# Attention into a gated feed-forward block on one core: token sums one by one on VectorE, one batch's last tokens earlier, two sigmoids ahead of two copies

## The chip, the cores and the metric

One Trainium2 chip, of which the kernel uses one core. The metric is the device time of one execution in microseconds (us). Engines are called as the profile calls them: PE is TensorE (PEld its weight loads), DVE is VectorE, ACT is ScalarE, POOL is GpSimd, and SP is SyncE, which here only issues DMA. Each engine works through its own instructions in program order; where the text says that an instruction stands "ahead of" another, this order on one engine is meant.

## The reference

Linear attention over 8 batches of 576 tokens with 8 heads of 64, a normalisation, and then a gated feed-forward block over all 4608 tokens of width 512.

```python
kv  = einsum('bhsd,bhse->bhde', k, v)              # per batch and head, 64x64
out = einsum('bhsd,bhde->bhse', q, kv)
x   = out / sqrt(mean(out*out) + 1e-6) * g_norm    # then as 4608 tokens x 512

g, val   = x @ w_gate, x @ w_val                   # 512 -> 1536
ffn_out  = (gelu(g) * val) @ w_out                 # 1536 -> 512
res_gate = sigmoid(x @ w_res)                      # 512 -> 512
result   = x + res_gate * ffn_out
```

## The kernel before

The feed-forward work goes in blocks of 512 tokens. Block b (0 to 7) holds the first 512 tokens of batch b; the last 64 tokens of all eight batches together make block 8. While PE works on block b, the attention of batch b+1 is done beside it. `plans[blk][slot]` lists what is added behind a slot of a block; slots 0 to NF-1 (NF = 12) are the gate and value products, NF and NF+1 the residual gates, NF+2 and NF+3 the two halves of the output product.

The output product of a block is done by a scheme with seven half-size products instead of eight (Strassen's, in Winograd's form). Each `prod` is 12 matmuls of 128x256 columns into a PSUM bank. "A", "D", "E" and "F" are banks; bank A takes four products one after the other and is read in between.

```python
def first_two():                               # slot NF+2
    prod(w["A"], a_of(blk, 1, 1), b_of(1, 1), True)
    nc.scalar.copy(out=w["E"], in_=w["A"])
    prod(w["D"], s_[0], wo_t[:, 0], True)
    nc.scalar.copy(out=w["d"], in_=w["D"])
    for j in range(NJ):
        m_sigmoid(j)                           # ACT: th = 0.5*th + 0.5

def pf(jj, src):                               # the gate: res = th * src, on DVE
    nc.vector.tensor_tensor(out=res_all[part(jj)], in0=th_all[part(jj)], in1=src, op=ALU.mult)

def fin(jj):                                   # the residual: res = res + t, on POOL
    nc.gpsimd.tensor_tensor(out=res_all[of], in0=res_all[of], in1=t_t[blk][of], op=ALU.add)

def others():                                  # slot NF+3
    prod(w["A"], s_[1], wo_t[:, 1], False)
    sub(nc.vector, w["F"], w["A"], w["d"], ALU.add)      # the sum into F
    prod(w["E"], a_of(blk, 1, 2), b_of(2, 1), False)
    pf((0, 0), w["E"])
    for f in rest:                                       # what the plan adds, all here
        f()
    prod(w["A"], s_[2], wo_t[:, 2], False)
    c22 = res_all[part((1, 1))]
    sub(nc.vector, c22, w["A"], w["d"], ALU.add)         # the sum out of A
    prod(w["F"], s_[3], b_of(2, 2), False)
    pf((0, 1), w["F"])
    fin((0, 0))
    prod(w["A"], a_of(blk, 2, 2), wo_t[:, 3], False)     # the last product
    pf((1, 1), c22)
    pf((1, 0), w["A"])
    fin((0, 1)); store(0); fin((1, 1)); fin((1, 0)); store(1)
```

In blocks 7 and 8 the gate and value products are done by the same scheme (`gv_group`, three groups of four column tiles each). It needs four sums and differences of quarters of the transposed tokens. They are made on DVE during the block before, among its output products:

```python
def token_sums(blk, eng):        # tile ts, 128x512 fp16 each; x_quadrant reads xT
    return [
        lambda: one(0, (0, 1), (0, 0)),    # used by product 5
        lambda: one(1, (1, 1), 0),         # reads sum 0; used by product 6
        lambda: one(2, (1, 1), (0, 1)),    # used by product 7
        lambda: one(3, (1, 0), 1),         # reads sum 1; used by product 4
    ]
# order of the words in a group: product 1g 1v, seed, 5g ... 6g ... plus F (DVE), 2g 2v, 7g, ...
```

The last 64 tokens of batches 2, 3, 5 and 7 (each with those of its partner) are scaled by `a_t` (DVE, o times the inverse root), multiplied by g in `a_x` (DVE) and sent through a transposing DMA (`d_xT`, SP queue):

```python
if rem:
    at(m, NF + 3, lambda: a_t(b, NJ))                    # m = b - 1; behind `others` of block m
...
if rem:
    at(m, NF + 3, lambda: a_x(b, NJ), lambda: d_xT(b, NJ, NJ + 1))
```

The last block has an output product of its own, with bank A split over two banks (`wa`):

```python
for e in range(2):
    prod(wa[e], a_of(blk, 1, 1), b_of(1, 1), True, (e,))
    nc.scalar.copy(out=we[:, one[e], :], in_=wa[e])
prod(wd, s_[0], wo_t[:, 0], True)
nc.scalar.copy(out=d, in_=wd)
for j in (2, 3, 0, 1):
    m_sigmoid(j)
for e in range(2):
    prod(wa[e], s_[1], wo_t[:, 1], False, (e,))
    sub(nc.vector, wf[:, one[e], :], wa[e], d[:, one[e], :], ALU.add)
sub(nc.gpsimd, u, th_all[part(2, 2, 1)], d, ALU.mult)              # u on POOL: tokens j = 2, 3
sub(nc.gpsimd, u, u, t_t[blk][part(2, 2, 1)], ALU.add)
prod(we, a_of(blk, 1, 2), b_of(2, 1), False)
gated(0, 2, 0, we)                       # DVE: res = th * src
plus(0, 2, 0, nc.gpsimd)                 # POOL: res = res + t
store(0, 2, 0, CH)
prod(wf, s_[3], b_of(2, 2), False)
gated(0, 2, 1, wf); plus(0, 2, 1, nc.gpsimd); store(0, 2, CH, C)
for e in range(2):
    prod(wa[e], s_[2], wo_t[:, 2], False, (e,))
    gated(2 + e, 1, 1, wa[e])
sub(nc.vector, res_all[of], res_all[of], u, ALU.add)               # DVE, reads u
store(2, 2, CH, C)
for e in range(2):
    prod(wa[e], a_of(blk, 2, 2), wo_t[:, 3], False, (e,))
    gated(2 + e, 1, 0, wa[e]); plus(2 + e, 1, 0, nc.vector)
store(2, 2, 0, CH)
```

Of the kernel before, what the change touches and what calls it, by code (L numbers as in the profile page):

```python
# [18 lines left out]
def kernel(  # L19
# [15 lines left out]
    nc = tc.nc  # L35
    P = nc.NUM_PARTITIONS
    B, H, S, D = q.shape
# [386 lines left out]
    def sub(eng, out_, in0, in1, op=ALU.subtract):  # L424
        eng.tensor_tensor(out=out_, in0=in0, in1=in1, op=op)  # L425
# [32 lines left out]
                    skip_group_check=True,  # L458
                )

    def out_by_products(blk, later, banks, rest=()):
        w = {}
        s_ = hid_sums

        def res(jj):
            for j in (2 * jj, 2 * jj + 1):
                m_res(blk, j, banks[j])

        def first_two():
            for n in ("D", "E", "F", "A"):  # L470
                w[n] = pmoe.tile([P, 2, CH], FP32, name="w" + n, bank=banks[n])
            w["d"] = finp.tile([P, 2, CH], FP32, tag="wd", bufs=1, name="wd")
# [7 lines that stand above are left out]
        def part(jj):  # L480
            return slice(None), slice(2 * jj[0], 2 * jj[0] + 2), slice(jj[1] * CH, (jj[1] + 1) * CH)

        def pf(jj, src):
            nc.vector.tensor_tensor(out=res_all[part(jj)], in0=th_all[part(jj)], in1=src, op=ALU.mult)  # L484

        def fin(jj):
            of = part(jj)
            nc.gpsimd.tensor_tensor(out=res_all[of], in0=res_all[of], in1=t_t[blk][of], op=ALU.add)  # L488

        def store(jj):  # L490
            dst = out[blk * S : blk * S + M0, :].rearrange("(p j) c -> p j c", j=NJ)
            js = slice(2 * jj, 2 * jj + 2)
            nc.sync.dma_start(out=dst[:, js, :], in_=res_all[:, js, :])

        def others():


            prod(w["A"], s_[1], wo_t[:, 1], False)
            sub(nc.vector, w["F"], w["A"], w["d"], ALU.add)
            prod(w["E"], a_of(blk, 1, 2), b_of(2, 1), False)  # L500
            pf((0, 0), w["E"])
            for f in rest:
                f()
            prod(w["A"], s_[2], wo_t[:, 2], False)
            c22 = res_all[part((1, 1))]
            sub(nc.vector, c22, w["A"], w["d"], ALU.add)
            prod(w["F"], s_[3], b_of(2, 2), False)
            pf((0, 1), w["F"])
            if not later:
                fin((0, 0))  # L510
            prod(w["A"], a_of(blk, 2, 2), wo_t[:, 3], False)
            pf((1, 1), c22)
            pf((1, 0), w["A"])
            if later:

                return
            fin((0, 1))
            store(0)
            fin((1, 1))
            fin((1, 0))  # L520
            store(1)

        if later:
            at(blk + 1, 5, lambda: fin((0, 0)))
            at(blk + 1, 6, lambda: fin((0, 1)), lambda: store(0))
            at(blk + 1, 9, lambda: fin((1, 0)))
            at(blk + 1, 10, lambda: fin((1, 1)), lambda: store(1))
        return [lambda: res(0), lambda: res(1), first_two, others]

    def out_last(blk, banks):  # L530

        s_ = hid_sums

        def bank(n, i):
            return pmoe.tile([P, n, CH], FP32, name="w", bank=i)

        def part(j, n, ch):
            return slice(None), slice(j, j + n), slice(ch * CH, (ch + 1) * CH)

        def gated(j, n, ch, src):  # L540
            of = part(j, n, ch)
            nc.vector.tensor_tensor(out=res_all[of], in0=th_all[of], in1=src, op=ALU.mult)

        def plus(j, n, ch, eng):
            of = part(j, n, ch)
            eng.tensor_tensor(out=res_all[of], in0=res_all[of], in1=t_t[blk][of], op=ALU.add)

        def store(j, n, c0, c1):
            for e, queue in enumerate((nc.sync, nc.scalar)):
                dst = out.rearrange("(j e s) c -> e s j c", e=2, s=S)[e, M0:S, j : j + n, c0:c1]  # L550
                queue.dma_start(out=dst, in_=res_all[e * R : (e + 1) * R, j : j + n, c0:c1])

        def run():
            wa = [bank(1, banks["A"][e]) for e in range(2)]
            wd, we, wf = [bank(2, banks[n]) for n in "DEF"]
            d = finp.tile([P, 2, CH], FP32, tag="wd", bufs=1, name="wd")
            u = attnp.tile([P, 2, CH], FP32, tag="sq", name="u")
            one = (slice(0, 1), slice(1, 2))
            for e in range(2):
                prod(wa[e], a_of(blk, 1, 1), b_of(1, 1), True, (e,))  # L560
                nc.scalar.copy(out=we[:, one[e], :], in_=wa[e])
            prod(wd, s_[0], wo_t[:, 0], True)
            nc.scalar.copy(out=d, in_=wd)
            for j in (2, 3, 0, 1):
                m_sigmoid(j)
            for e in range(2):
                prod(wa[e], s_[1], wo_t[:, 1], False, (e,))
                sub(nc.vector, wf[:, one[e], :], wa[e], d[:, one[e], :], ALU.add)
            sub(nc.gpsimd, u, th_all[part(2, 2, 1)], d, ALU.mult)
            sub(nc.gpsimd, u, u, t_t[blk][part(2, 2, 1)], ALU.add)  # L570
            prod(we, a_of(blk, 1, 2), b_of(2, 1), False)
            gated(0, 2, 0, we)
            plus(0, 2, 0, nc.gpsimd)
            store(0, 2, 0, CH)
            prod(wf, s_[3], b_of(2, 2), False)
            gated(0, 2, 1, wf)
            plus(0, 2, 1, nc.gpsimd)
            store(0, 2, CH, C)
# [3 lines that stand above are left out]
            of = part(2, 2, 1)  # L582
            sub(nc.vector, res_all[of], res_all[of], u, ALU.add)
# [3 lines that stand above are left out]
                gated(2 + e, 1, 0, wa[e])  # L587
                plus(2 + e, 1, 0, nc.vector)
            store(2, 2, 0, CH)

        return [lambda: [m_res(blk, j, banks[j]) for j in range(NJ)], run]
# [479 lines left out]
    def plan_attn(b):  # L1071


        rem = pair(b) is not None
        m = b - 1
        begin = [lambda: attn_begin(b), lambda: d_qT(b)]
        if rem:
            begin.append(lambda: d_rem_qT(b))
        if b == 2:
            at(m, 0, lambda: by_token(b))  # L1080
            at(m, 1, *begin)
            k0, o0, n0 = 4, 6, 9
        else:
            if b == 3:
                amid_out[m - 1] = [lambda: by_token(b), *begin]
            else:
                at(m - 1, NF, lambda: by_token(b))
                at(m - 1, NF + 1, *begin)
            k0, o0, n0 = 1, 3, 7
        at(m, k0, lambda: a_kv(b))  # L1090
        if b + 1 < B:
            at(m, k0 + 1, lambda: load_behind(b))
        if rem:
            at(m, o0 - 1, lambda: a_rem_o(b))
            at(m, o0 + 2, lambda: a_ss(b, NJ))
        at(m, o0, lambda: a_o(b))
        for j in range(NJ):
            at(m, o0 + j // 2, lambda j=j: a_ss(b, j))
        at(m, n0, lambda: a_norm(b, 0, NJ + rem))
        n0 += 1 if b == 2 else 2  # L1100
        for j in range(NJ):
            at(m, NF if b == 2 and j > 1 else n0 + j // 2, lambda j=j: a_t(b, j))
        if rem:
            at(m, NF + 3, lambda: a_t(b, NJ))
        for j in range(NJ):
            at(m, NF if b == 2 else n0 + 1, lambda j=j: a_x(b, j))
        at(m, NF, lambda: d_xT(b, 0, NJ))
        if rem:
            at(m, NF + 3, lambda: a_x(b, NJ), lambda: d_xT(b, NJ, NJ + 1))

    units = [(n, g) for g in range(NF // GF) for n in "gv"]
    all_sums = [f for u in units for f in weight_sums(u, nc.vector)]
# [28 lines left out]
    for blk in range(B + 1):  # L1141
# [10 lines left out]
        else:  # L1152
# [15 lines left out]
            for j, f in enumerate(sums_in.get(blk, ())):  # L1168
                plan.setdefault(SUM_SLOTS[j], []).append(f)
            if blk + 1 in LAST:  # L1170
                amid_out.setdefault(blk, []).extend(token_sums(blk + 1, nc.vector))

            def products(blk=blk, outs=outs):
                s_rest(blk)
# [2 lines left out]
                if blk + 1 == LAST[0]:  # L1177
                    out_at[blk].update({j: pattn.turn[j] for j in range(NJ)})
                if blk < B:
                    outs.extend(out_by_products(blk, blk == 1, out_at[blk], amid_out.get(blk, ())))  # L1180
                else:
                    outs.extend(out_last(blk, out_at[blk]))

# [57 lines left out]
```

## Time and profile before

| | before |
|---|---|
| time, median of 3 runs | 343.77 us (343.67 to 343.92) |
| span of the profiled execution | 346.3 us |
| granted TensorE clock, mean | 0.998 |
| output products of block 6, 7, 8 (start of the first) | 264.98, 298.46, 330.70 us |
| first group of block 7 | 275.53 us |
| HBM read and written | 38.80 and 9.44 MB |

A profiled execution is a little longer than a timed one; differences between two profiles are read, not their absolute length. In a timeline line the columns are the start in us from the span's start, the duration in us, the engine, the source line, the operation, the tiles written and read with their shapes and types, the number of instructions merged into the line, and in brackets the idle time of the engine just before with the instruction that ended it. The line numbers are of kernel.py; L425 is the helper `sub` and so stands for many sums, which are told apart by their tiles. `w` followed by a letter is a bank of the output product, `ts` the token sums, `osb` the result `res_all`, `th` the gate, `wd` the tile d, and `w` alone any bank of block 8. A matmul's end is modelled, so the pace of PE is taken from one start to the next.

### The profile page before, as it was taken

How to read it: one execution, taken by the hardware profiler on the slowest of the kernel's cores; microseconds unless marked ns; L12 is line 12 of the kernel's file. 1: busy time of each engine (PE TensorE's matmuls, PEld its weight loads, DVE VectorE, ACT ScalarE, POOL GpSimd, SP SyncE). 2: the span in 40 equal slices, each digit the busy share in tenths (PEclk: the TensorE clock that was granted, in tenths of full speed). 3: DMA queues.
4: the chain of work that ended last, by engine and by line, in shares of the span. 5: the costliest groups of instructions: out<-in, count | busy, mean ns of one | idle time of the engine just before them, and what ended most of it. 6: DMA issues, size and time to landing. Idle time of an engine off the chain costs nothing.

```text
span 346.3 us, 6525 instructions
## 1 busy us (share of the span) xinstructions
PE 330.3 (95%) x2576; PEld 202.9 (59%) x2576; DVE 258.3 (75%) x498; ACT 161.3 (47%) x289; POOL 110.1 (32%) x127
## 2 busy tenths in 40 slices
PE   8779999999999999999999999999999899989992
PEld 3534454444854476447644674466546778778882
DVE  5474529749958988878677978796799787677854
ACT  3355365454526361536163525353544366636750
POOL 2692160892043207400650066005000431151222
PEclk9999999999999999999999999999999999999999
DMA  7999999359389363983498349935103030011004
GB/s 242 281 182 204 194 203 169 86 132 182 44 148 180 122 77 107 188 94 70 140 172 87 61 123 178 105 61 139 62 0 61 2 137 2 2 51 73 0 2 121
DMA packets 76688, 38.82 MB, mean 112 GB/s; under 512 B 42098, under 2 KB 74354, under 8 KB 76658
## 3 DMA queue, kind: packets, MB, share of 16 engines
q0 software_dynamic: 38752, 17.17, 39.5%
q1 hardware_dynamic: 37328, 20.71, 22.0%
q10 hardware_dynamic: 578, 0.52, 0.4%
q8 instruction: 20, 0.33, 0.4%
q14 instruction: 10, 0.08, 0.1%
HBM read 38.80 MB, written 9.44 MB: 139 GB/s over the span
## 4 chain that ended last, share of the span: by engine, by line
PE 86%; DVE 7%; DMA 2%; ACT 2%; issue 1%; SPq 1%; DVEq 0%
PE gps L357 21%; PE vps L357 20%; PE wA L452 9%; PE rps L377 8%; PE Av L682 3%; PE Ag L682 3%; PE fps L394 3%; PE wD L452 3%; PE w L452 2%; DMA hid_s<-in_v_dram 2%; PE wF L452 2%; PE wE L452 2%; PE kvp L208 2%; PE Fv L682 2%; PE Fg L682 2%; DVE ts L425 1%
## 5 line engine op out<-in xcount | busy, mean ns | idle before, releaser
L345 ACT ACTIVATE ge<-gps 128x512 f16<-128x512 f32 x84 | 50.0, 597 | 98.5 <-PE gps L357 97.7
L357 PE MATMUL vps<-xT,wv 128*128 128x512 f16 x328 | 84.2, 379 | 0.8 <-DVE hid L346 0.8
L357 PE MATMUL gps<-xT,wg 128*128 128x512 f16 x328 | 84.3, 380 | 0.0
L346 DVE TENSOR_TENSOR hid<-ge,vps 128x512 f16<-128x512 f16 x84 | 57.4, 684 | 32.6 <-PE vps L357 28.7
L488 POOL TENSOR_TENSOR osb<-osb,t 128x512 f32<-128x512 f32 x28 | 36.2, 1311 | 138.9 <-DVE osb L484 133.1
L357 PEld LDWEIGHTS <-wv 128*128 128x128 f16 x328 | 32.1, 98 | 39.7 <-issue 1.1
L357 PEld LDWEIGHTS <-wg 128*128 128x128 f16 x328 | 30.7, 98 | 34.5 <-issue 0.2
L452 PEld LDWEIGHTS <-hid_s 128*128 128x128 f16 x384 | 37.6, 98 | 4.5 <-issue 0.2
L452 PEld LDWEIGHTS <-hid 128*128 128x128 f16 x288 | 28.1, 98 | 8.2 <-issue 3.5
L377 PE MATMUL rps<-wr,xT 128*128 128x512 f16 x144 | 32.5, 379 | 0.0
L386 ACT ACTIVATE th<-rps 128x512 f32<-128x512 f32 x36 | 21.5, 597 | 16.4 <-PE rps L377 16.4
L377 PEld LDWEIGHTS <-xT 128*128 128x128 f16 x144 | 14.1, 98 | 16.6
L245 DVE TENSOR_REDUCE ss<-sq 128x8 f32<-128x512 f32 x32 | 20.6, 680 | 2.9 <-ACT sq L243 2.7
L682 PEld LDWEIGHTS <-ws 128*128 128x128 f16 x192 | 18.8, 98 | 3.3 <-issue 1.2
L452 PE MATMUL wA<-wo_ts,hid_s 128*128 128x256 f16 x168 | 20.6, 273 | 0.0
L391 ACT ACTIVATE th<-th 128x512 f32<-128x512 f32 x36 | 19.8, 622 | 0.0
L303 DVE TENSOR_TENSOR t<-op,ny 128x512 f16<-128x512 f32 x28 | 17.9, 683 | 0.1
L243 ACT ACTIVATE sq<-op 128x512 f32<-128x512 f32 x28 | 15.3, 596 | 4.5 <-PE op L226 4.2
L317 DVE TENSOR_TENSOR t<-t,g 128x512 f16<-128x512 f16 x36 | 16.2, 500 | 0.1
L425 DVE TENSOR_TENSOR hid_s<-hid 128x1536 f16<-128x1536 f16 x16 | 15.3, 954 | 0.2
L719 POOL TENSOR_TENSOR hid<-ge,c 128x512 f16<-128x512 f16 x6 | 7.0, 1164 | 25.6 <-ACT ge L713 25.6
L452 PE MATMUL wA<-wo_ts,hid 128*128 128x256 f16 x84 | 10.3, 272 | 2.3 <-DVE osb L425 2.3
(172 smaller groups left out, 481.4 us busy)
## 6 DMA issues: line engine op xcount, KB each, us to landing
out_dram<-osb SPq DMA_DIRECT2D x14, 512.0 KB, 2.6
qraw<-in_q_dram POOLq DMA_DIRECT2D x7, 512.0 KB, 7.8
k<-in_k_dram POOLq DMA_DIRECT2D x7, 512.0 KB, 9.5
v<-in_v_dram POOLq DMA_DIRECT2D x7, 512.0 KB, 11.3
wg<-in_moe_w_gate_dram POOLq DMA_DIRECT2D x2, 512.0 KB, 8.6
wv<-in_moe_w_val_dram POOLq DMA_DIRECT2D x2, 512.0 KB, 9.4
wo<-in_moe_w_out_dram POOLq DMA_DIRECT2D x2, 512.0 KB, 14.2
out_dram<-osb SPq DMA_DIRECT2D x4, 256.0 KB, 2.8
```

Source lines behind the costliest of these rows:

```text
L245: nc.vector.tensor_reduce(out=out_, in_=sq, op=ALU.add, axis=mybir.AxisListType.X)
L303: nc.vector.tensor_tensor(out=t, in0=o, in1=scale, op=ALU.mult)
L345: nc.scalar.activation(out=ge, in_=gps, func=AF.Gelu)
L346: nc.vector.tensor_tensor(out=hids[blk][:, f, :], in0=ge, in1=vps, op=ALU.mult)
L357: nc.tensor.matmul(ps[:, j0 * P : j1 * P], lhsT=w[:, cc, :], rhs=xT_t[blk][:, j0:j1, cc, :], start=(cc == 0 and j0 == 0), stop=(cc == NP - ...
L377: nc.tensor.matmul(rps, lhsT=xT_t[blk][:, j, cc, :], rhs=wr16[:, cc, :], start=(cc == 0), stop=(cc == NP - 1),)
L386: nc.scalar.activation(out=th, in_=rps, func=AF.Tanh, scale=0.5)
L391: nc.scalar.activation(out=th, in_=th, func=AF.Copy, scale=0.5, bias=0.5)
L425: eng.tensor_tensor(out=out_, in0=in0, in1=in1, op=op)
L452: nc.tensor.matmul(ps[:, e - es[0], :], lhsT=a[:, f, e * P : (e + 1) * P], rhs=b[:, f, :], start=(start and e == es[0] and f == 0), stop=( ...
L488: nc.gpsimd.tensor_tensor(out=res_all[of], in0=res_all[of], in1=t_t[blk][of], op=ALU.add)
L682: nc.tensor.matmul(out_[:, r, :], lhsT=lhsT, rhs=rhs, start=(first and r == 0 and c == 0), stop=(c == 1), skip_group_check=True,)
```

## The change

Three instruction streams are reordered. Nothing is computed that was not computed before, and no buffer changes.

- The four token sums for block 7 (during block 6) and for block 8 (during block 7) no longer stand in a row behind the first gate product. Each goes to a place of its own among the DVE instructions of the output product: sum 0 behind the sum into F, sum 2 behind the first gate, sum 1 behind the sum out of A, sum 3 behind the gate of F. The order 0, 2, 1, 3 keeps what the sums read of each other.
- The scaling of the last tokens of batch 7, with its transposing DMA, goes from behind the output product of block 6 to a place within it, ahead of the sum into F. For batches 2, 3 and 5 it stays where it was.
- In the last block the sigmoids of tokens j = 2 and 3 go ahead of the two copies of `wa` into `we`. Those of j = 0 and 1 stay behind the copy of d.

The purpose is to put DVE work into gaps where DVE waits for PE or ACT, so that the sums that free a bank for PE are not held up by it, and to let u on POOL start earlier.

```diff
-    def out_by_products(blk, later, banks, rest=()):
+    def out_by_products(blk, later, banks, amid):
+        def aside(ahead_of):
+            for f in amid.get(ahead_of, ()):
+                f()
@@ others()
             prod(w["A"], s_[1], wo_t[:, 1], False)
+            aside("F")
             sub(nc.vector, w["F"], w["A"], w["d"], ALU.add)
+            aside("00")
             prod(w["E"], a_of(blk, 1, 2), b_of(2, 1), False)
             pf((0, 0), w["E"])
-            for f in rest:
-                f()
+            aside("22")
             prod(w["A"], s_[2], wo_t[:, 2], False)
             c22 = res_all[part((1, 1))]
             sub(nc.vector, c22, w["A"], w["d"], ALU.add)
+            aside("01")
             prod(w["F"], s_[3], b_of(2, 2), False)
             pf((0, 1), w["F"])
             if not later:
                 fin((0, 0))
+            aside("11")
             prod(w["A"], a_of(blk, 2, 2), wo_t[:, 3], False)
@@ out_last
             for e in range(2):
                 prod(wa[e], a_of(blk, 1, 1), b_of(1, 1), True, (e,))
+            for j in (2, 3):
+                m_sigmoid(j)
+            for e in range(2):
                 nc.scalar.copy(out=we[:, one[e], :], in_=wa[e])
             prod(wd, s_[0], wo_t[:, 0], True)
             nc.scalar.copy(out=d, in_=wd)
-            for j in (2, 3, 0, 1):
+            for j in (0, 1):
                 m_sigmoid(j)
@@ plan_attn
-                amid_out[m - 1] = [lambda: by_token(b), *begin]
+                amid_out[m - 1] = {"22": [lambda: by_token(b), *begin]}
...
-        if rem:
-            at(m, NF + 3, lambda: a_t(b, NJ))
...
-        if rem:
-            at(m, NF + 3, lambda: a_x(b, NJ), lambda: d_xT(b, NJ, NJ + 1))
+        last = [lambda: a_t(b, NJ), lambda: a_x(b, NJ), lambda: d_xT(b, NJ, NJ + 1)]
+        if rem and b + 1 == B:
+            amid_out.setdefault(m, {})["F"] = last
+        elif rem:
+            at(m, NF + 3, *last)
@@ the blocks
             if blk + 1 in LAST:
-                amid_out.setdefault(blk, []).extend(token_sums(blk + 1, nc.vector))
+                for ahead_of, f in zip(("00", "01", "22", "11"), token_sums(blk + 1, nc.vector)):
+                    amid_out.setdefault(blk, {}).setdefault(ahead_of, []).append(f)
```

More of the change, by code (lines that the diff above doesn't have):

```diff
@@ L1179, in products @@
                 if blk < B:
-                    outs.extend(out_by_products(blk, blk == 1, out_at[blk], amid_out.get(blk, ())))
+                    outs.extend(out_by_products(blk, blk == 1, out_at[blk], amid_out.get(blk, {})))
                 else:
```

## The prediction

> **What bounds the kernel now.** I read the page's busy shares first, then the chain that ended last, then what the matmul engine waits for in the last third, and last the timeline around each such wait.
>
> ```profile
> PE 330.3 (95%) x2576; PEld 202.9 (59%) x2576; DVE 258.3 (75%) x498; ACT 161.3 (47%) x289; POOL 110.1 (32%) x127
> ...
> PE 86%; DVE 7%; DMA 2%; ACT 2%; issue 1%; SPq 1%; DVEq 0%
> ```
>
> PE is busy for 95% of the span and holds 86% of the chain, so only places where PE stands still can give time back, and the end, where PE is already through. From 200 us on, PE has three waits, all on DVE (columns: who waits, for whom, us in total, times, longest):
>
> ```profile
> PE wA L452 <- DVE osb L425: 2.3, 2, 1.2
> PE Ag L682 <- DVE Fg L703: 0.8, 1, 0.8
> ```
>
> They sit exactly where the change reaches. The first, in the output products of block 6 (timeline: start us, duration, engine, line, operation, tiles):
>
> ```profile
> 269.18 0.70 DVE L425 TENSOR_TENSOR wF<-wA,wd 128x512 f32<-128x512 f32 x1 [1.27 <-PE wA L452]
> 270.58 0.69 DVE L484 TENSOR_TENSOR osb<-th,wE 128x512 f32<-128x512 f32 x1 [0.71 <-ACT th L391]
> 271.19 0.42 DVE L425 TENSOR_TENSOR ts<-xT 128x512 f16<-128x512 f16 x1
> 271.35 1.27 POOL L488 TENSOR_TENSOR osb<-osb,t 128x512 f32<-128x512 f32 x1 [29.09 <-DVE osb L484]
> 271.52 1.47 PE L452 MATMUL wF<-wo,hid_s 128*128 128x256 f16 x12
> 271.64 1.26 DVE L425 TENSOR_TENSOR ts<-xT,ts 128x512 f16<-128x512 f16 x1
> 272.82 0.41 DVE L425 TENSOR_TENSOR ts<-xT 128x512 f16<-128x512 f16 x1
> 273.16 0.41 DVE L425 TENSOR_TENSOR ts<-xT,ts 128x512 f16<-128x512 f16 x1
> 273.50 0.68 DVE L425 TENSOR_TENSOR osb<-wA,wd 128x512 f32<-128x512 f32 x1
> ...
> 274.23 1.47 PE L452 MATMUL wA<-wo_ts,hid 128*128 128x256 f16 x12 [1.23 <-DVE osb L425]
> ```
>
> Four token sums (ts) stand in a row on DVE, in front of the sum that reads bank wA (273.50). Until wA is read, PE may not start its last product into it, though product F had ended. And DVE stood idle before this row twice: 1.27 us ahead of the sum into F, 0.71 us ahead of the first gating product.
>
> The second place is the first group of block 7, where the last tokens' scaling (o to t, then t times g) runs on DVE in front of the sum Fg:
>
> ```profile
> 276.41 1.63 DVE L303 TENSOR_TENSOR t<-o,ny 128x512 f16<-128x512 f32 x1
> 278.08 1.27 DVE L317 TENSOR_TENSOR t<-t,g 128x512 f16<-128x512 f16 x1
> 278.59 0.60 PE L682 MATMUL Ev<-xT,wv 128*128 128x256 f16 x4
> 279.27 0.69 DVE L703 TENSOR_TENSOR Fg<-Ag,d 128x512 f32<-128x512 f32 x1
> 280.00 0.60 PE L682 MATMUL Ag<-ts,ws 128*128 128x256 f16 x4 [0.82 <-DVE Fg L703]
> ```
>
> The third is the end, block 8, where PE runs without a gap from 330.87 to its last matmul, and ACT, POOL and DVE set the finish:
>
> ```profile
> 333.52 0.58 ACT L563 COPY wd<-w 128x512 f32<-128x512 f32 x1 [0.90 <-PE w L452]
> 334.01 2.19 ACT L391 ACTIVATE th<-th 128x512 f32<-128x512 f32 x4
> 335.24 1.28 POOL L425 TENSOR_TENSOR u<-th,wd 128x512 f32<-128x512 f32 x1 [7.31 <-ACT th L391]
> 337.70 2.27 POOL L546 TENSOR_TENSOR osb<-osb,t 128x512 f32<-128x512 f32 x2
> 339.29 1.23 DVE L425 TENSOR_TENSOR osb<-osb,u 128x512 f32<-128x512 f32 x1
> ```
>
> POOL starts u only after the second sigmoid, is busy without a pause until 339.97, and the DVE sum at 339.29 takes 1.23 us beside it.
>
> **What the Trainium skill says.** "SBUF — State Buffer", section "Who interferes with whom": a DVE instruction with two SBUF inputs contends with a GpSimd instruction that reads SBUF, and the one issued first holds the shared ports to its end; one with a PSUM input does not. The trace agrees: the token sum with two SBUF inputs takes 0.41 us alone and 1.26 us just after POOL began at 271.35; t<-o,ny takes 0.68 us at 98.05 with POOL idle and 1.63 us here; the sum out of wA (a PSUM input) stays between 676 and 693 ns over all seven blocks, POOL busy or not. "Perfetto Trace Analysis", section "Tensor Engine Instruction", calls DVE and ACT strict FIFO and the end of a matmul modelled: four sums ahead of the wA sum hold it although its input is there, and I measure PE from start to start. "VectorE: DVE Perf Modes", section on the perf-mode tier table, gives tensor_tensor its 2x mode for 16-bit SBUF operands and 1x for fp32: 0.41 against 0.69 us here for 512 elements.
>
> **The change, part by part.** No operation is added or dropped. Four parts:
>
> 1. Sums one by one, block 6. PE's pace for a product of 12 matmuls is 1.31 us from start to start (block 5, which has no token sums: F at 236.39, last product at 237.70). Without the wait the last product would start at 271.52 + 1.31 = 272.83; it started at 274.23. Cost: **1.40 us**. Does the new order remove all of it? The sum into F ends at 269.88; token sum 0 (0.42) runs to 270.3 in the old idle gap, as the gating product behind it waits for ACT until 270.58 anyway. Its input, the transpose issued at 264.39, lands 4.2 us later, 268.6. Then gating, to 271.27; token sum 2 in the very place where sum 0 stood, 271.2 to 271.6, issued just before POOL begins; the wA sum waits for PE's product, which ends at about 271.52 + 0.16 = 271.7, and runs to 272.4. That is 0.4 us before PE asks for wA. Token sum 1 then meets the end of POOL's instruction (272.62) and ends near 272.95, while the gating of F waits for product F until 273.0. Sum 3 follows and is first needed by product 4 of the next group. So the whole 1.40 should go.
>
> 2. Sums one by one, block 7, same pattern: F starts at 305.01, so 306.32 against 307.61: **1.29 us**.
>
> 3. Last tokens of batch 7 ahead of the sum into F, block 6. In the old place: four Ev matmuls at 278.59 pace 0.44 us, so the next would start at 279.03 and started at 280.00, 0.97 us; these four then take 0.60 instead of 0.44, 0.16 more. Cost **1.13 us**. In the new place DVE is free from 266.95 + 0.96 = 267.91. POOL has been idle for 29 us there, so the short durations apply: 0.68 + 0.42, start to end 267.95 to 269.09 (98.05 to 99.19 at block 2). The sum into F waits for PE until 269.18. It fits with 0.09 us to spare, and behind that there is another 0.33 us, since PE asks for wA again only at 270.21 and the sum into F ended at 269.88.
>
> 4. Two sigmoids ahead of the copies, block 8. Four sigmoids take 2.19 us, so two take 1.1. ACT is free at 331.5 after the last tanh; sigmoids to 332.6, copies of 0.36 each to 333.35, still ahead of the copy of d (333.52, set by PE); PE wants wA back at 333.3 and its other half at 333.95, so it does not wait. Then u needs only d, 333.52 + 0.58 = 334.1, instead of 335.24: POOL's u and its addition end near 336.6. Its two closing additions are then bound by the DVE products: 336.9 to 338.05 and, after the product at 337.46, 338.15 to 339.3. The DVE sum with u at 339.29 runs beside nothing: 0.69 or so instead of 1.23. All that follows it on DVE, to the last store, comes about **0.52 us** earlier (the next product at 339.92 instead of 340.44).
>
> Sum: 1.40 + 1.29 + 1.13 + 0.52 = 4.34 us. PE is the chain in between (group after group without a gap), so the savings add. 343.77 - 4.34 = 339.43; I add 0.1 for semaphore slack: **339.5 us**, 1.2% less.
>
> **The rivals.** (a) The wait moves in front of F: the last tokens' two operations meet something on POOL or a late operand and take 1.63 + 1.27 as before. Then the sum into F would start at 270.9 instead of 269.18, PE's next product into wA about 1.4 us late, and part 1 is eaten: some 340.9. For it: only 0.42 us of slack. Against: POOL's 29 idle us. (b) Token sum 2 loses the ports to POOL, whose addition becomes ready at the same moment. It then ends near 272.9, the wA sum near 273.5, PE starts 0.75 us late, in both blocks: 1.5 less saved, about 341.0. Against: in both blocks sum 0 stood in this place and took 0.42. (c) The end is set by the stores: 1 MB leaves between 340.2 and 345.1 at 221 to 240 GB/s, so an earlier last store could queue behind the others: part 4 worth nothing, 339.95. Against: the earlier three stores move forward too. (d) Copies of the last block come too late for PE: at worst 0.1 to 0.3 us.
>
> **Range and chances.** One of (a) or (b) failing wholly gives about 341; (c) and (d) cost half a microsecond; better than 4.9 us would need a gain I do not see. So 338.8 to 340.9. A gain above 2% (6.9 us) has no source: 0.02. Slower by 2% would need a new stall of 7 us: 0.01.
>
> **What would show it.** The PE waits on osb L425 and on Fg should both be gone after 260 us, the last products of blocks 6 and 7 start 1.31 us after F; no new PE wait ahead of product A or F. The slow 1.63 and 1.27 become about 0.68 and 0.42. Token sums: one of four in each block longer than 0.42, and not number 2. In block 8 u starts within 0.1 us of the end of the copy of d (before: 1.14 us after it), and the 1.23 falls to 0.7. Wrong would be a PE wait of 0.3 us or more on wF or wA, or a last store no earlier against PE's last matmul.

## The result and the profile after

The changed kernel takes 339.93 us (median of 4 runs, 339.0 to 340.75) against 343.72 us before (4 runs, 343.55 to 343.92): a ratio of 0.9889, 95% interval 0.9856 to 0.9921. The forecast was 339.5 us with a range of 338.8 to 340.9.

The two profiles must not be compared by their spans. These are 346.3 and 337.3 us, 9.0 us apart, and almost half of that has nothing to do with the change: it lies in the opening, where both kernels have the same instructions. Nor is a profiled execution longer as such: the one before took 348.22 us, 4.5 us above the median of its kernel, the one after 339.26 us, which is below its median. The first residual product of block 0 starts at 44.42 us in the profile before and at 40.02 us in the one after. From there on I compare section by section: the time from the first residual product (PE, tile rps) of one block to that of the next, which the trace of any version gives to 0.01 us. The end is that of the last instruction in the trace (346.30 and 337.35 us).

| section, us | before | after | difference |
|---|---|---|---|
| opening, to block 0 | 44.42 | 40.02 | other loads' arrival, see below |
| each section from block 0 to block 6 | 40.02, 36.37, 35.23, 35.24, 34.94, 35.24 | 40.03, 36.38, 35.23, 35.24, 34.94, 35.24 | 0.0 |
| block 6 to 7 | 33.55 | 31.03 | -2.52 |
| block 7 to 8 | 32.24 | 30.96 | -1.28 |
| block 8 to the end | 19.05 | 18.28 | -0.77 |

The sections that the change touches give back 2.52 + 1.28 + 0.77 = 4.57 us; the others behind the opening stay within 0.01 us. The last section is the least certain: over the five profiled kernels that keep the old order of the sigmoids it takes 18.89 to 19.05 us, over those that differ from the changed kernel only ahead of block 8 18.23 to 18.28.

The page after, busy shares and chain by engine:

```profile
PE 326.6 (97%) x2576; PEld 200.9 (60%) x2576; DVE 255.4 (76%) x498; ACT 161.5 (48%) x289; POOL 109.3 (32%) x127
...
PE 90%; DVE 4%; DMA 3%; issue 0%; ACT 0%; POOL 0%; SPq 0%; DVEq 0%
```

PE's share of the chain rises from 86 to 90%, DVE's falls from 7 to 4%: DVE left the path in blocks 6 and 7, and what remains of it lies elsewhere, at the end for one. From 225 us to the end the view of PE's waits has no line any more. The timeline of block 6 after, at the place shown of before:

```profile
263.44 0.69 DVE L303 TENSOR_TENSOR t<-o,ny 128x512 f16<-128x512 f32 x1
264.16 0.43 DVE L317 TENSOR_TENSOR t<-t,g 128x512 f16<-128x512 f16 x1
264.80 0.70 DVE L425 TENSOR_TENSOR wF<-wA,wd 128x512 f32<-128x512 f32 x1 [0.21 <-PE wA L452]
265.40 0.41 DVE L425 TENSOR_TENSOR ts<-xT 128x512 f16<-128x512 f16 x1
266.20 0.69 DVE L488 TENSOR_TENSOR osb<-th,wE 128x512 f32<-128x512 f32 x1 [0.39 <-ACT th L391]
266.81 0.42 DVE L425 TENSOR_TENSOR ts<-xT 128x512 f16<-128x512 f16 x1
266.97 1.27 POOL L492 TENSOR_TENSOR osb<-osb,t 128x512 f32<-128x512 f32 x1 [29.08 <-DVE osb L488]
267.15 1.47 PE L452 MATMUL wF<-wo,hid_s 128*128 128x256 f16 x12
267.40 0.69 DVE L425 TENSOR_TENSOR osb<-wA,wd 128x512 f32<-128x512 f32 x1 [0.17 <-issue]
268.01 0.52 DVE L425 TENSOR_TENSOR ts<-xT,ts 128x512 f16<-128x512 f16 x1
268.46 1.47 PE L452 MATMUL wA<-wo_ts,hid 128*128 128x256 f16 x12
...
269.26 0.42 DVE L425 TENSOR_TENSOR ts<-xT,ts 128x512 f16<-128x512 f16 x1
269.42 1.27 POOL L492 TENSOR_TENSOR osb<-osb,t 128x512 f32<-128x512 f32 x1 [1.18 <-DVE osb L488]
269.60 1.64 DVE L488 TENSOR_TENSOR osb<-th,osb 128x512 f32<-128x512 f32 x1
```

The scaling takes 0.69 + 0.43 us (before: 1.63 + 1.27) and DVE still waits 0.21 us for PE ahead of the sum into F. Each token sum stands in a place of its own, and the last product starts 268.46 - 267.15 = 1.31 us behind F, PE's own pace. The last line is one that I did not foresee: the gate out of c22 (`pf((1, 1), c22)`) takes 1.64 us now, beside POOL's second addition. Before, DVE began it 0.16 us ahead of POOL (274.85), and it took 0.68 us:

```profile
274.69 0.68 DVE L484 TENSOR_TENSOR osb<-th,osb 128x512 f32<-128x512 f32 x1
```

It is not on the path here. In the first group of block 7 (its banks Ag, Ev, Fg and so on play the parts of A, E and F in the gate and value products), Fg no longer keeps PE waiting:

```profile
272.22 0.70 DVE L713 TENSOR_TENSOR Fg<-Ag,d 128x512 f32<-128x512 f32 x1 [0.38 <-PE Ag L692]
272.82 0.60 PE L692 MATMUL Ev<-xT,wv 128*128 128x256 f16 x4
273.26 0.60 PE L692 MATMUL Ag<-ts,ws 128*128 128x256 f16 x4
```

From Ev to the next Ag 0.44 us, where it was 1.41. And block 8:

```profile
323.22 1.14 ACT L391 ACTIVATE th<-th 128x512 f32<-128x512 f32 x2
324.26 0.77 ACT L571 COPY w<-w 128x256 f32<-128x256 f32 x2
325.34 0.59 ACT L573 COPY wd<-w 128x512 f32<-128x512 f32 x1 [0.32 <-PE w L452]
325.82 1.15 ACT L391 ACTIVATE th<-th 128x512 f32<-128x512 f32 x2
326.01 1.27 POOL L425 TENSOR_TENSOR u<-th,wd 128x512 f32<-128x512 f32 x1 [6.26 <-ACT wd L573]
328.79 2.41 POOL L553 TENSOR_TENSOR osb<-osb,t 128x512 f32<-128x512 f32 x2 [0.28 <-DVE osb L549]
331.11 0.69 DVE L425 TENSOR_TENSOR osb<-osb,u 128x512 f32<-128x512 f32 x1
...
333.41 0.59 SPq L558 DMA_DIRECT2D out_dram<-osb  x1
```

The two sigmoids and the copies fit in front of the copy of d, which still waits 0.32 us for PE. u starts 0.08 us behind d, and the sum with u takes 0.69 us instead of 1.23. The last line is the issue of the last store; before, it was

```profile
342.13 0.59 SPq L551 DMA_DIRECT2D out_dram<-osb  x1
```

so 342.13 - 327.25 = 14.88 us into the section, and now 333.41 - 319.07 = 14.34.

### The profile page after: what moved, and what is told of

Same layout as the page of the kernel before. It is cut to its first block, busy times and chain, and to the rows that moved or that the text cites. A ratio compares the mean times of both kernels' runs of the same rounds, so it can differ in the third digit from the quotient of the medians.

```text
span 337.3 us, 6523 instructions
## 1 busy us (share of the span) xinstructions
PE 326.6 (97%) x2576; PEld 200.9 (60%) x2576; DVE 255.4 (76%) x498; ACT 161.5 (48%) x289; POOL 109.3 (32%) x127
## 4 chain that ended last, share of the span: by engine, by line
PE 90%; DVE 4%; DMA 3%; issue 0%; ACT 0%; POOL 0%; SPq 0%; DVEq 0%
PE gps L357 21%; PE vps L357 20%; PE wA L452 11%; PE rps L377 8%; PE fps L394 3%; PE Av L692 3%; PE Ag L692 3%; PE wE L452 3%; PE wD L452 3%; PE wF L452 3%; PE w L452 2%; DMA hid_s<-in_v_dram 2%; PE kvp L208 2%; PE Fv L692 2%; PE Fg L692 2%; DMA kf<-in_k_dram 2%
## 5 line engine op out<-in xcount | busy, mean ns | idle before, releaser
L492 POOL TENSOR_TENSOR osb<-osb,t 128x512 f32<-128x512 f32 x28 | 35.3, 1277 | 138.0 <-DVE osb L488 132.4
L317 DVE TENSOR_TENSOR t<-t,g 128x512 f16<-128x512 f16 x36 | 15.4, 478 | 0.1
L394 PE MATMUL fps<-wo,hid 128*128 128x512 f16 x48 | 11.2, 379 | 0.0
```

What stands on the lines that cost most here:

```text
L394: nc.tensor.matmul(fps, lhsT=hids[blk][:, f, j * P : (j + 1) * P], rhs=wo16[:, f, :], start=(f == 0), stop=(f == NF - 1))
```

## The experiments

What each version gave, by section; "to 7" is block 6 to 7, "to 8" block 7 to 8, "end" block 8 to the end. Ratios are to the kernel before on the same chip. The forecasts counted "end" from the start as the chain of waits shows it, about 0.17 us later than the timeline's start used here, and from spans rounded to 0.1 us (18.88 and 18.07 there are 19.05 and 18.28 here). The time of three_times is the median of its five fast runs; its profile is of the sixth, a slow one (345.31 us, mean granted clock 0.989), whose sections outside block 6 to 7 agree with those of the changed kernel to 0.02 us.

| version | time, us | ratio (95% interval) | to 7 | to 8 | end |
|---|---|---|---|---|---|
| before | 343.7 | 1 | 33.55 | 32.24 | 19.05 |
| sums_only | 341.67 | 0.9944 (0.9928 to 0.9961) | 32.91 | 30.96 | 18.89 |
| last_only | 342.55 | 0.9963 (0.9951 to 0.9976) | 32.41 | 32.24 | 18.97 |
| sig_only | 342.92 | 0.9977 (0.9967 to 0.9986) | 33.54 | 32.24 | 18.23 |
| pool_later | 341.87 | 0.9944 (0.9932 to 0.9956) | 32.71 | 31.40 | 18.91 |
| sums_fin_later | 341.02 | 0.9914 (0.9886 to 0.9942) | 31.95 | 30.96 | 18.95 |
| after_again | 339.17 | 0.9862 (0.9843 to 0.9881) | 31.03 | 30.96 | 18.27 |
| two_at_22 | 340.60 | 0.9919 (0.9894 to 0.9944) | 31.74 | 31.57 | 18.25 |
| three_times | 340.40 | 0.9914 (0.9884 to 0.9945) | 31.87 | 30.97 | 18.28 |
| best | 338.32 | 0.9840 (0.9823 to 0.9858) | 31.02 | 30.97 | 18.18 |

### sums_only: the token sums alone

```diff
-        if rem and b + 1 == B:
-            amid_out.setdefault(m, {})["F"] = last
-        elif rem:
+        if rem:
             at(m, NF + 3, *last)
```

and the sigmoids of block 8 back in the old order.

> Only the token sums are moved; the last tokens stay behind the output product of block 6 and the sigmoids behind the copy of d. Theory 1, the parts add as in the prediction: 2.7 us less than before; block 6 to 7 (first residual product to first residual product) takes 33.55 - 1.40 = 32.15 us and the wait for Fg in the first group of block 7 stays at about 1.0 us from start to start. Theory 2, the parts lean on each other: PE enters block 7 1.4 us earlier, but DVE does not, as its second-to-last gate is held by POOL (1.64 us instead of 0.68 in the changed kernel). The scaling of the last tokens then begins about 2.1 us after PE enters block 7 instead of 0.9, so the wait for Fg grows to about 2 us and this version saves only some 1.6 us: 0.3 in block 6 to 7 and 1.3 in block 7 to 8.

Block 7 to 8 gives the 1.28 us of the prediction, but block 6 to 7 only 33.55 - 32.91 = 0.64 us instead of 1.40. The wait for Fg grew, as the second theory has it, though less of the gain was lost than it said (0.3 us was to be left). Timeline of sums_only:

```profile
270.97 1.27 POOL L492 TENSOR_TENSOR osb<-osb,t 128x512 f32<-128x512 f32 x1 [1.18 <-DVE osb L488]
271.15 1.65 DVE L488 TENSOR_TENSOR osb<-th,osb 128x512 f32<-128x512 f32 x1
...
273.31 1.27 DVE L303 TENSOR_TENSOR t<-o,ny 128x512 f16<-128x512 f32 x1
...
274.37 0.60 PE L689 MATMUL Ev<-xT,wv 128*128 128x256 f16 x4
274.62 1.26 DVE L317 TENSOR_TENSOR t<-t,g 128x512 f16<-128x512 f16 x1
...
276.54 0.60 PE L689 MATMUL Ag<-ts,ws 128*128 128x256 f16 x4 [1.57 <-DVE Fg L710]
```

PE could have started Ag at 274.37 + 0.44 = 274.81 and started at 276.54: 1.73 us late, and 0.16 more for the first four at 0.60 us, 1.89 together, where it was 1.13. The difference, 0.76 us, is just what is missing: 1.40 - 0.76 = 0.64. So the parts do not add; the sums bring PE to block 7 earlier, and the last tokens' scaling, if left there, eats half of it.

### sums_fin_later: the same, with POOL idle at the gate out of c22

```diff
-            fin((0, 1))
-            store(0)
-            fin((1, 1))
+            if blk + 1 not in LAST:
+                fin((0, 1))
+                store(0)
+                fin((1, 1))
+            else:
+                fin((1, 1))
+                fin((0, 1))
+                store(0)
             fin((1, 0))
```

> The version with the sums alone, with one more change in blocks 6 and 7: POOL's addition for tokens 0 and 1, second half, stands behind the one for tokens 2 and 3, second half, so that POOL is idle when DVE makes the gate out of c22 (1.65 us beside POOL there). Theory, POOL's hold of that gate is why the sums alone bring 0.64 us in block 6 to 7 instead of 1.40: without it the gate takes 0.69 us, the last tokens' scaling begins some 0.9 us earlier against PE, and the wait for Fg falls from 1.89 us (start to start, with the slow first four matmuls) to about 1.1: 32.1 us in block 6 to 7 instead of 32.91. Rival, the scaling is held by POOL wherever it starts, and block 6 to 7 stays above 32.6 us.

```profile
270.87 0.69 DVE L488 TENSOR_TENSOR osb<-th,osb 128x512 f32<-128x512 f32 x1
271.64 4.02 POOL L492 TENSOR_TENSOR osb<-osb,t 128x512 f32<-128x512 f32 x3 [2.12 <-DVE osb L488]
...
274.10 0.60 PE L694 MATMUL Ev<-xT,wv 128*128 128x256 f16 x4
...
275.30 0.60 PE L694 MATMUL Ag<-ts,ws 128*128 128x256 f16 x4 [0.60 <-DVE Fg L715]
```

The gate takes 0.69 us, and Ag comes 275.30 - 274.54 = 0.76 us late instead of 1.73. Block 6 to 7 takes 31.95 us. One swap of two additions on POOL, with no other change, is worth 32.91 - 31.95 = 0.96 us here: POOL's hold of one gate was the link between the parts. Each of the two operations of the scaling takes 1.27 us beside POOL in both versions, so what differs between these two is when the scaling starts, not how long it lasts.

### last_only: the last tokens alone

```diff
-                for ahead_of, f in zip(("00", "01", "22", "11"), token_sums(blk + 1, nc.vector)):
+                for ahead_of, f in zip(("22",) * 4, token_sums(blk + 1, nc.vector)):
```

and the sigmoids back.

> Only the scaling of the last tokens of batch 7 goes ahead of the sum into F; the four sums stay in a row. Prediction's step: the wait for Fg is gone and nothing takes its place, 1.1 us less than before; the sum into F still starts with PE's product (its idle time before it falls from 1.27 to about 0.2 us), and the two waits on the sum out of A stay at 1.2 us. Rival: the two operations delay the sum into F, PE waits ahead of its third product into A, and the gain is below 0.5 us.

Block 6 to 7 takes 32.41 us, 1.14 less than before (prediction: 1.13). The sum into F still waits for PE, and the waits on the sum out of A stay as they were:

```profile
264.41 0.70 DVE L425 TENSOR_TENSOR wF<-wA,wd 128x512 f32<-128x512 f32 x1 [0.21 <-PE wA L452]
```

```profile
PE wA L452 <- DVE osb L425: 2.3, 2, 1.2
```

Rival (a) of the prediction falls in this place. sums_only and last_only together give 0.64 + 1.14 = 1.78 us in this section, both at once 2.52.

### sig_only: the two sigmoids alone

The change's own lines of `out_last`, in the kernel before.

> Only the two sigmoids of the last block go ahead of the copies. Prediction's step: from the first residual product of block 8 to the last addition on DVE 13.73 us instead of 14.26, the sum with u 0.69 us instead of 1.23, no PE wait; the time 0.5 us less than before, or up to 0.8 if the stores come through quicker as well. Rival: the stores set the end, and the time from the first residual product of block 8 to the end of the span stays at 18.9 us although DVE is done 0.5 us earlier.

The timeline of sig_only, block 8:

```profile
334.82 0.69 DVE L425 TENSOR_TENSOR osb<-osb,u 128x512 f32<-128x512 f32 x1
...
337.12 0.60 SPq L551 DMA_DIRECT2D out_dram<-osb  x1
```

Block 8 to the end takes 18.23 us, 0.82 less than before; block 6 to 8 is untouched. DVE's part is the predicted one: the sum with u is short, and the last store is issued 337.12 - 322.78 = 14.34 us into the section as in the changed kernel, 0.54 earlier than before. The remaining 0.28 us lies behind the issue: from it to the end 4.17 us before, 3.89 here. But that time varies. Over the five profiled kernels with the old order it is 4.01 to 4.17 us (mean 4.08), over four with the new order (sig_only, the changed kernel twice, two_at_22) 3.89 to 3.94 (mean 3.92). So the change brings 0.54 + 0.16 = 0.70 us at the end on average, and the pair before and after, 0.77, lies a little above that. The three stores ahead of the last are issued 0.73, 0.60 and 0.59 us earlier, so they move a little further ahead than the last one. That the last store then finds the DMA engines freer fits this and the next tail below, but was not isolated.

### pool_later: the row of sums without POOL beside it

```diff
             pf((0, 1), w["F"])
-            if not later:
+            if not later and blk + 1 in LAST:
+                fin((0, 1))
+                fin((0, 0))
+            elif not later:
                 fin((0, 0))
@@
-            fin((0, 1))
+            if blk + 1 not in LAST:
+                fin((0, 1))
             store(0)
```

> The kernel before, with one thing changed in blocks 6 and 7: POOL's first addition (tokens 0 and 1, first half) stands behind its second, so that POOL does not work while DVE goes through its row of four token sums. Theory 1, the hold of the ports by POOL makes most of the wait: the row takes about 1.5 us instead of 2.4, the sum out of A starts 0.86 us earlier, and the PE wait falls from 1.40 and 1.29 us (start to start) to about 0.5 in each block: 1.7 us less than before. Theory 2, the number of operations makes the wait: the second sum stays long or PE's wait does not change by more than 0.2 us in each block.

The second sum of the row, which took 1.26 us before, and then PE's waits from 225 us on:

```profile
267.12 0.42 DVE L425 TENSOR_TENSOR ts<-xT,ts 128x512 f16<-128x512 f16 x1
```

```profile
PE Ag L686 <- DVE Fg L707: 0.8, 1, 0.8
PE wA L452 <- DVE osb L425: 0.7, 2, 0.4
```

Both sections fall by 0.84 us (33.55 to 32.71, 32.24 to 31.40). Of the 1.40 and 1.29 us that the row cost, 0.84 came from POOL's hold of one sum of four, and only the rest from the row being four sums long. Theory 1 holds.

### two_at_22: two sums in one place

```diff
-                for ahead_of, f in zip(("00", "01", "22", "11"), token_sums(blk + 1, nc.vector)):
+                for ahead_of, f in zip(("22", "01", "22", "11"), token_sums(blk + 1, nc.vector)):
```

> The changed kernel, with token sum 0 taken back to a place directly ahead of sum 2, behind the first gate. So two sums in a row there, 0.42 us more DVE work ahead of the sum out of A. Theory of the ports: the first of them takes 0.42 us, the second begins after POOL and is held to about 1.2, the sum out of A ends 0.6 us after PE wants the bank: PE waits about 0.6 us in both blocks, 1.2 us more than the changed kernel. Theory of the count: 0.42 us more, of which the slack takes nearly all: no PE wait above 0.15 us, and the same time.

```profile
266.95 1.71 DVE L425 TENSOR_TENSOR ts<-xT 128x512 f16<-128x512 f16 x2
...
268.59 0.68 DVE L425 TENSOR_TENSOR osb<-wA,wd 128x512 f32<-128x512 f32 x1
...
269.32 1.47 PE L452 MATMUL wA<-wo_ts,hid 128*128 128x256 f16 x12 [0.56 <-DVE osb L425]
```

The two sums take 1.71 us instead of about 0.8, the second alone 1.38. The sections grow by 0.71 and 0.61 us. One sum in this place is free and a second costs 0.66 us on average, more than its own 0.42: the place behind the first gate has room for one, because POOL starts right behind it (at 267.12 us here). This is rival (b) of the prediction, made to happen: it put 0.75 us in each block on a sum that loses the ports there.

### three_times: how much the place ahead of F holds

```diff
-            amid_out.setdefault(m, {})["F"] = last
+            amid_out.setdefault(m, {})["F"] = [last[0], last[0], *last]
```

> The changed kernel, with the first scaling of the last tokens (o to t) done three times in place of once ahead of the sum into F: the same values are written again, 2 x 0.61 us more DVE work. From the trace the sum into F starts 0.21 us after DVE is free and PE asks for its bank 0.34 us after its end, so 0.55 us are free; the rest, about 0.7 us, should show as a PE wait ahead of its third product into A and as 0.7 us more time in block 6 to 7. Rival: the gap in which DVE waits is wide enough for more, and nothing changes; or the later sums are pushed into POOL's hold as well and it costs more than 1.2 us.

```profile
271.88 1.47 PE L452 MATMUL wA<-wo_ts,hid_s 128*128 128x256 f16 x12 [0.70 <-DVE wF L425]
```

Block 6 to 7 grows by 0.84 us (31.87 against 31.03). PE waits 0.70 us by the profile. The reckoning from the slack gave 0.7, from two more operations of 0.61 us; from the start of the three to the operation behind them it took 2.17 us (268.63 to 270.80), where it took 0.72 with one (263.44 to 264.16), and 1.45 - 0.55 = 0.90 us comes closer to the 0.84. Rival (a) of the prediction is real, but needs some 0.5 us more DVE work than the change puts there.

### after_again: the spread of the changed kernel

No edit.

> The changed kernel once more, for its own spread. In its four runs so far it took 339.0, 339.3, 340.6 and 340.8 us, while the kernel before stayed within 0.4 us. Theory 1: the two levels come from the opening, in which the first loads arrive; then everything from the first residual product of block 6 to the end repeats to 0.1 us (31.03, 30.96 and 18.07 us), and only what lies ahead of it varies. Theory 2: a wait comes and goes in the changed part; then one of these three lengths differs by more than 1 us between executions.

The three sections are 31.03, 30.96 and 18.27 us, the same to 0.01 us as in the first profile, and the opening took 41.45 us instead of 40.02: a span of 338.7 against 337.3. Over all profiles, the first residual product of block 0 starts between 39.68 (last_only) and 44.42 us (before), and at 45.23 in three_times, with the same program up to there. In the five late openings (41.33 us and more) the first big load of v takes 7.2 to 7.8 us from issue to landing, in the six early ones (40.18 us at most) 5.5 to 5.8. That fits the first 1.5 us; what made the two latest openings some 3 us later still was not followed. So the first theory holds for the two executions of this kernel that have a profile. The median of this series, 339.17 us, is 4.59 us below the 343.76 us of the kernel before on the same chip, against 4.57 us by sections; the first series' 3.79 us had two of four runs above 340.5 us.

### best: two more reorderings

```diff
-                    plan.setdefault(3 + j, []).append(g)     # t times g of block 1, in block 2
+                    plan.setdefault(1 + j, []).append(g)
@@ out_last
-            sub(nc.vector, res_all[of], res_all[of], u, ALU.add)
+            sub(nc.gpsimd, res_all[of], res_all[of], u, ALU.add)
@@
                 gated(2 + e, 1, 0, wa[e])
-                plus(2 + e, 1, 0, nc.vector)
+            plus(2, 2, 0, nc.vector)
```

> The changed kernel with two more reorderings of the same kind. (1) In block 2 the four products of block 1's tokens with g are done two slots earlier, where DVE is idle, so that POOL's additions end before DVE's chain of short operations for the norm; the PE wait of 0.95 us (start to start) in block 2 should go, wholly or most of it. (2) In the last block the sum with u goes from DVE to POOL, and the last two additions are one of double width: the last addition ends 0.35 us earlier against PE's last product. Together 1.0 to 1.3 us less than the changed kernel. Rival: the earlier products take DVE's time from the squares' sums of the next batch and only move the wait; or the sum on POOL holds the ports when DVE makes its last addition, and the end is later.

It takes 338.32 us, 0.85 below after_again on the same chip; by their ratios to the kernel before the intervals of the two overlap slightly. The sections: block 0 to 1 is unchanged, block 1 to 2 falls from 36.38 to 35.42 us, block 2 to 3 from 35.23 to 34.94, the end from 18.28 to 18.18. That is 1.35 us by sections, a little more than the forecast, and 0.85 us by medians, less than it; as most of these runs have no profile, how much of the 0.5 us between the two is the openings stays open. In the changed kernel, one operation of DVE's chain for the norm is held by POOL, and PE waits behind the chain:

```profile
108.78 2.27 POOL L492 TENSOR_TENSOR osb<-osb,t 128x512 f32<-128x512 f32 x2 [0.36 <-DVE t L317]
...
110.01 1.08 DVE L276 TENSOR_SCALAR ny<-nm 128x40 int32<-128x40 int32 x1
...
113.84 1.02 PE L357 MATMUL vps<-xT,wv 128*128 128x512 f16 x4 [0.79 <-DVE hid L346]
```

In best the same operation is short, and PE has no wait after the opening:

```profile
109.50 0.18 DVE L276 TENSOR_SCALAR ny<-nm 128x40 int32<-128x40 int32 x1
```

The second part brought less than thought. Timeline of best, block 8:

```profile
329.74 1.26 POOL L425 TENSOR_TENSOR osb<-osb,u 128x512 f32<-128x512 f32 x1
...
330.95 0.69 DVE L553 TENSOR_TENSOR osb<-osb,t 128x512 f32<-128x512 f32 x1
...
331.72 0.60 SPq L558 DMA_DIRECT2D out_dram<-osb  x1
```

The last store is issued 331.72 - 317.66 = 14.06 us into the section, 0.28 earlier than in the changed kernel, but the end comes only 0.10 us earlier. The third store waits for POOL now and goes out 0.68 us ahead of the last one, where it was 1.50 ahead (331.04 and 331.72; 331.91 and 333.41).

## Why the prediction was right, point by point

**Steps 1 and 3, block 6: right in sum, mixed up in parts.** 1.40 + 1.13 = 2.53 was said, 2.52 came. Both readings of the cost as it stood were right, and so was the order in which the new DVE instructions run. The step "so the savings add" is wrong for these two: with the sums alone the section gives 0.64 us, with the last tokens alone 1.14, together 1.78, and the 1.40 needs the last tokens out of the way. The sum came out because the change does both. sums_fin_later shows why: POOL's addition holds the gate out of c22. The prediction followed DVE's row up to token sum 3 and stopped there, since nothing behind it was on PE's path any more. With the scaling still behind it, as in sums_only, the same sum would be wrong by 0.76 us.

**Step 2, block 7: right.** 1.29 said, 1.28 measured, and it came whole in sums_only, since no scaling follows there.

**The places of the sums: right.** Sum 2 takes 0.42 us where sum 0 stood; sum 1 meets POOL and takes 0.52 and 0.46 us; the sum out of A ends 0.4 us ahead of PE's wish (268.09 against 268.46). The slack ahead of F was said to be 0.09 + 0.33 us; it is 0.21 and 0.34, and three_times overdraws it as it should.

**Step 4, block 8: right in mechanism, a little too small.** The term "0.52" held for the issue of the last store (0.54), but the end came 0.77 us earlier in the two profiles, and 0.70 on average over the kernels with the old and the new order. The mis-sized term is the time from the last issue to the end, taken as fixed and measured at 4.08 and 3.92 us on average. Rival (c), stores that set the end, thus turned out the other way round in the change, and shows in its predicted direction in best.

**The time.** 4.34 us were summed and 339.43 expected, with 339.5 written; 4.57 us came by sections, and 339.93 and 339.17 us as medians of two series. Their profiled executions differ by 1.39 us in the span and by 1.43 in the opening, so not in the change. That 339.5 lies between the two medians is in part luck, as the opening differs between executions by more than the 0.23 us by which the sum was short.

## What to carry to other kernels

When an engine is a queue in front of the bottleneck, ask of each gap what fits in it and what other engine begins just behind it: here one sum fitted behind the first gate and a second cost more than its length, because POOL's addition came between. Before adding up the gains of two reorderings, follow the row behind the first one to where it next meets the bottleneck; freeing an engine earlier can lengthen the next wait by more than half the gain. And compare profiles by sections between marks that both have: here the opening alone moved the span by 4.7 us between before and last_only.

## What the runs showed of the hardware that was not expected

The hold of a DVE operation by POOL shows inside its duration and not as a wait: the same gate is 0.68 or 1.64 us, a token sum 0.41, 1.26 or 1.38, a 128x40 operation 0.18 or 1.08. So the view of waits blames the DVE operation for the whole of it, and the stretched line beside a POOL line is the only sign. POOL's own additions of 128x512 fp32 into `osb` are not all alike either: 1.15 or 1.16 us in 21 of 34 places of the changed kernel, 1.26 to 1.60 in the others. At the gate out of c22 the order of the two starts goes with which one is long: DVE first, 0.68 us and POOL's addition 1.53 (before); POOL first, 1.27 us and DVE's gate 1.64 (after). Exchanging two of them cost PE nothing in pool_later and sums_fin_later and took 0.84 and 0.96 us off a section.

In the two profiles of the changed kernel the sections behind the opening repeat to 0.02 us (mean granted clock 0.997 in both). The same instructions of the opening, in which PE waits for the first loads, take 39.68 to 44.42 us over the profiles, and those behind the last store's issue 4.01 to 4.17 us over five kernels with the same tail.
